# Gated linear attention with a SwiGLU gate: four F blocks ahead instead of five, masked states and key sums by PSUM bank, one reciprocal for a query tile's factors, and the first down weights split without waiting

## The chip, the cores and the metric

The kernel runs on one core of one Trainium2 chip. The time is device microseconds from start to end of one execution; the figure for the kernel before is the median of three runs, 1640.54 us (1640.27 to 1640.99). TensorE multiplies matrices out of SBUF into PSUM (eight banks). VectorE, ScalarE and GpSimd work elementwise; GpSimd cannot reach PSUM. DMA transfers are issued from the queues of SP, ScalarE and GpSimd. Each engine carries out its own instructions in a fixed order and waits on semaphores for the others.

## The reference

One sequence of S = 2048 rows with D = 576 columns, H = 32 heads of 18, and a feed-forward width F = 4608.

```
xn = layernorm(x)
# A: linear attention with a feature map of two softmaxes
q, k, v = split(xn @ wqkv)                      # 32 heads of 18
pq, pk = q @ w_phi, k @ w_phi                   # per head
phi_q = concat(softmax(pq), softmax(-pq))       # 36 features
phi_k = concat(softmax(pk), softmax(-pk))
kv = sum over rows of phi_k^T v;  z = sum over rows of phi_k
o  = (phi_q @ kv) / (phi_q @ z + 1e-6)
s  = o @ wo
# B: SwiGLU
g = silu( (silu(xn @ w_gate) * (xn @ w_up)) @ w_down )
out = x + s * g
```

## The kernel before

Every fp32 operand of a large product is split into a rounded part and a rest (`split`, L57: a ScalarE copy for the first, a VectorE subtraction for the second), and three products of the parts replace one. The rows of x are kept transposed in eight tiles X (`XB`), four for each half of the rows. The program has these stages.

**Opening and keys.** Layernorm, transposes, weights folded with w_phi, then `k_tile` for each of 16 row tiles: the products with the key weights, `softmax_parts` (maximum and minimum, two exponentials on ScalarE, the head sums `sm` and their reciprocals on VectorE), and `kv_step`, which adds phi_k^T v into three PSUM banks `kvp` (four 126-wide blocks in the first two, two 72-wide ones in the third). A column of ones beside v gives the key sums z.

**The seam between keys and queries** (L491 to L515). The key sums are copied out of the banks to `zc` (L500, one column at a time), spread over all partitions by matmuls with the identity (L506) and copied to `zb` (L509). The ten state blocks are masked to their heads (`km`, L513) and split into `KVH` and `KVL`.

**Queries** (L559 to L619). For each row tile `q_tile` multiplies with the query weights, takes the softmax parts, forms ez = e times zb, its head sums y, and from them the factors of numerator and denominator; the last operation on e (L577) applies them. `numer` transposes two such tiles (`pt`, L588) and multiplies with the states (`po`, L594); `project` multiplies with wo (`p`, L614), copies the result on ScalarE (`so`, L618) and stores it.

**Gate, up and down.** F is cut into NF = 36 blocks of 128. The first EARLY blocks are computed ahead, in the plain form: `early_tile` makes, for each of four tiles of 512 rows, 14 matmuls of 512 columns for the gate and 14 for the up product (xw, L92), a Silu on ScalarE, a product on VectorE, and stores h to DRAM. These blocks are given out as filler for TensorE beside the attention stages; the last of them (L1020, L1026) stands between the last projection and the gate stage. All other blocks go through `gate_up` (L727), which computes both products for both tiles of one half of the rows with seven products of seven matmuls (L706) instead of eight; its weights are loaded to `ld`, combined on GpSimd (`ts`, L693 to L696), split to `w`, and kept in DRAM (`w_dram`) for the second half of the rows. In the first two of them (`opening` 0 and 1) the sum xp is copied to SBUF by ScalarE (`snap`, L735) before the next product may add to it. The down product works on pairs of blocks, again by seven products (`strassen`): GpSimd forms the differences of h and of the down rows (`td`, L916 to L923), `prep` splits them to `hh` and `dw`, and `item` multiplies (`pd`, L831).

The program is written with tiles; a scheduler puts each engine's instructions in an order of its own, by priority and by when it expects operands. `tc.high_priority()` lifts an instruction in that order, `tc.issue_after(x)` holds one back until x has been placed. The first down rows lie in the space of `acc` (`first_rows`, loaded at L1024), and for the first step of the first pairs `prep` holds all VectorE work back behind `anchor`, the last product of a gate block:

```
with tc.issue_after(anchor[-1].ins) if first and i == 0 and part == 0 else ExitStack():
    for n, g in enumerate(pairs):
        h, w = f(g)
        hs.append(split_h(h))
        split(w2[:, n, 0], w2[:, n, 1], w)
```

Of the kernel before, what the change touches and what calls it, by code (L numbers as in the profile page):

```python
# [17 lines left out]
P = 128  # L18
# [11 lines left out]
EARLY = 5  # L30
# [7 lines left out]
def heads(ap):  # L38
    return ap.rearrange("p (h d) -> p h d", d=DH)
# [7 lines left out]
def gated_hedgehog_kernel(ctx: ExitStack, tc, x, w_qk, w_v, w_phi, wo, w_gu, w_tail, w_down, ident_in, mask_in, out):  # L47
# [78 lines left out]
    with ExitStack() as att:  # L126
# [9 lines left out]
        with ExitStack() as wst:  # L136
# [136 lines left out]
            def softmax_parts(ps, e):  # L273
# [12 lines left out]
                nc.vector.reciprocal(sm, sm)  # L286
# [114 lines left out]
            def k_tile(t):  # L401
                i0, j0, cols = block(t)
                pk = kps.tile([P, 2, 512], F32, name="p2")
                for i in range(2):
                    w = slice(i * HALF, (i + 1) * HALF)
                    xw(pk[:, i, 0:HALF], i0, j0, cols, KVWH[:, :, :, w], KVWL[:, :, :, w], True)
                phi = kk.tile([P, 2 * D], F32, name="phi", bufs=2)
                sm = softmax_parts(pk, phi)
                nc.vector.tensor_mul(heads(phi), heads(phi), spread(sm, 2 * H))
                return phi  # L410
# [80 lines left out]
        with ExitStack():  # L491
# [4 lines left out]
            zc = qc.tile([GW, 2 * NG], F32, name="zc")  # L496
            for i in range(3):
                for j in range(4 if i < 2 else 2):
                    w = GROUPS[(4 * i + j) // 2][1]
                    nc.scalar.copy(zc[0:w, 4 * i + j:4 * i + j + 1], kvp[i][0:w, j, w:w + 1])  # L500
            for s in range(2):
                for a, m, name in ((0, 4, ("p2", "vw")[s]), (4, 1, ("vy", "vx")[s])):
                    o, w = GROUPS[a]
                    zp = kps.tile([P, 512], F32, name=name)
                    for g in range(a, a + m):
                        nc.tensor.matmul(zp[:, (g - a) * GW:(g - a) * GW + w],  # L506
                                         zc[0:w, 2 * g + s:2 * g + s + 1].to_broadcast([w, P]), ident[0:w, 0:w],
                                         start=True, stop=True)
                    nc.scalar.copy(zb[:, s * D + o:s * D + o + m * w], zp[:, 0:m * w])  # L509
            for i in range(2 * NG):  # L510
                o, w = GROUPS[i // 2]
                km = qc.tile([GW, GW], F32, name="km", bufs=2)
                nc.vector.tensor_mul(km[0:w, 0:w], kvp[i // 4][0:w, i % 4, 0:w],  # L513
                                     mask.rearrange("p h d -> p (h d)")[0:w, 0:w])
                split(KVH[0:w, i, 0:w], KVL[0:w, i, 0:w], km[0:w, 0:w])  # L515
# [7 lines left out]
        with ExitStack() as qst:  # L523
# [35 lines left out]
            def q_tile(t):  # L559
                i0, j0, cols = block(t)  # L560
                pq = qps.tile([P, 2, 512], F32, name="p2")
                for i in range(2):
# [3 lines left out]
                r = softmax_parts(pq, e)  # L566
# [4 lines left out]
                nc.vector.tensor_mul(y, y, r)  # L571
                den = qk.tile([P, H], F32, name="den")
                nc.vector.scalar_tensor_tensor(den, y[:, 0:H], DEN_EPS, y[:, H:], op0=ALU.add, op1=ALU.add)
                nc.vector.reciprocal(den, den)
                nc.vector.tensor_mul(r.rearrange("p (s h) -> p s h", s=2), r.rearrange("p (s h) -> p s h", s=2),
                                     den.unsqueeze(1).to_broadcast([P, 2, H]))
                last_e.append(nc.vector.tensor_mul(heads(e), heads(e), spread(r, 2 * H)))  # L577
# [20 lines left out]
            def project(b, oh, ol, last):  # L598
                for j in range(QS // P):
# [3 lines left out]
                    for i in range(2):  # L603
# [14 lines left out]
                        nc.scalar.copy(so, ps[:, 0:HALF])  # L618
# [273 lines left out]
    def strassen(i, pairs, part, first):  # L892
# [65 lines left out]
        for f in ((p1, p7), (p4, p5, p6, p2, p3))[part]:  # L958
            hs, ws = [], []

            def prep(f=f, hs=hs, ws=ws):
                w2 = fq.tile([P, 2, 2, HALF], F32R, name="dw", bufs=3)
                with tc.issue_after(anchor[-1].ins) if first and i == 0 and part == 0 else ExitStack():
                    for n, g in enumerate(pairs):
                        h, w = f(g)
                        hs.append(split_h(h))
                        split(w2[:, n, 0], w2[:, n, 1], w)
                        ws.append(w2[:, n])
# [134 lines left out]
```

## Time and profile before

| | |
|---|---|
| median of three runs | 1640.54 us |
| profiled execution | 1640.45 us, its span 1638.7 us |
| mean granted TensorE clock | 0.997 |
| keys to queries, the first query matmul | at 232.4 us |
| end of the last projection | at 488.8 us |
| first matmul of the gate, up and down stage | at 513.5 us |

A line of the groups gives the source line, the engine, the operation, the tile written and those read, shapes and count, then busy us, mean ns of one, and idle time before with what ended it. A line of a timeline begins with its start in us from the span's start and its duration; a bracket at its end holds the idle time of the engine before it and what ended that. A line of the view of waits gives who waited for whom, then us in total, times, and the longest. A line of the view by windows gives, for a stretch, the busy time of TensorE, its weight loads, VectorE, ScalarE and GpSimd with their counts, then the granted TensorE clock, the DMA share and GB/s. Matmuls are pipelined, so that their recorded durations overlap.

### The profile page before, as it was taken

The numbers are of one execution on the slowest core, as the hardware profiler recorded it, in microseconds if no ns is written. First come the engines' busy times: TensorE is split into PE (matmuls) and PEld (weight loads), VectorE is DVE, ScalarE is ACT, GpSimd is POOL, SyncE is SP. The second block draws the span as 40 slices with busy tenths as digits, with TensorE's granted clock in tenths as the row PEclk, the third lists the DMA queues.
The fourth block names the chain that finished last, engine by engine and source line by source line (L and its number), as shares of the span: only waits on it lengthen the run. The fifth ranks groups of instructions, "written<-read, shape, count | busy, mean of one in ns | idle before, by whom it ended". The sixth has DMA issues, their size and how long they took to land.

```text
span 1638.7 us, 25220 instructions
## 1 busy us (share of the span) xinstructions
PE 1604.5 (98%) x9385; PEld 1429.4 (87%) x9385; DVE 1175.5 (72%) x1735; ACT 723.8 (44%) x1407; POOL 655.3 (40%) x699
## 2 busy tenths in 40 slices
PE   6999999999999999999999999999999999999997
PEld 5899997999988888888888888888888888888886
DVE  7667768989863778778777778825676766666578
ACT  5533344454433554544444544455433333333334
POOL 3385661342303455455545355313233323133132
PEclk9999999999999999999999999999999999999999
DMA  8622234433329545555554454685454655555445
GB/s 285 206 80 78 78 130 128 117 112 96 93 94 330 202 167 175 178 178 168 179 181 164 174 197 152 223 293 149 140 162 130 201 182 177 166 181 180 140 115 174
DMA packets 121741, 268.47 MB, mean 164 GB/s; under 512 B 12786, under 2 KB 53362, under 8 KB 119826
## 3 DMA queue, kind: packets, MB, share of 16 engines
q1 hardware_dynamic: 106652, 246.49, 46.0%
q0 software_dynamic: 3072, 11.02, 2.5%
q10 hardware_dynamic: 11894, 9.35, 1.8%
q8 instruction: 74, 1.21, 0.3%
q14 instruction: 49, 0.40, 0.1%
HBM read 167.19 MB, written 99.61 MB: 163 GB/s over the span
## 4 chain that ended last, share of the span: by engine, by line
PE 90%; DVE 3%; DMA 3%; POOL 1%; issue 1%; ACT 1%; SPq 0%; ACTq 0%; POOLq 0%; DVEq 0%
PE px L706 24%; PE pd L831 24%; PE pw L706 12%; PE py L706 6%; PE p L92 6%; PE pe L92 5%; PE p L614 4%; PE po L594 2%; PE kvp L295 2%; PE vx L383 1%; PE pt L588 1%; PE vw L383 1%; DMA sraw<-in_A_w_v 1%; DMA xn<-in_A_x 1%; DMA x_dram<-xr 1%
## 5 line engine op out<-in xcount | busy, mean ns | idle before, releaser
L831 PEld LDWEIGHTS pd<-dw,hh 128*128 128x128 f32 x3048 | 432.4, 188 | 26.2 <-DVE dw L59 2.9
L831 PE MATMUL pd<-dw,hh 128*128 128x288 f32 x3048 | 448.5, 297 | 3.8 <-DVE dw L59 2.1
L706 PE MATMUL px<-X,w 128*128 128x512 f32 x1488 | 384.4, 393 | 0.2 <-ACT s L735 0.2
L706 PEld LDWEIGHTS px<-X,w 128*128 128x128 f32 x1488 | 270.6, 188 | 52.2 <-ACT s L735 2.4
L706 PE MATMUL pw<-X,w 128*128 128x512 f32 x732 | 188.7, 393 | 0.0
L706 PEld LDWEIGHTS pw<-X,w 128*128 128x128 f32 x732 | 137.0, 189 | 30.5
L740 DVE TENSOR_TENSOR s<-pw,s 128x512 f32<-128x512 f32 x124 | 85.0, 687 | 101.0 <-ACT s L735 90.3
L956 DVE TENSOR_TENSOR acc<-pd,acc 128x576 f32<-128x576 f32 x128 | 96.2, 752 | 83.6 <-PE pd L831 83.5
L735 ACT COPY s<-px 128x512 f32<-128x512 f32 x124 | 72.6, 585 | 158.3 <-PE px L706 158.3
L92 PE MATMUL pe<-X,wh 128*128 128x512 f32 (+1 forms) x380 | 121.5, 401 | 5.2 <-ACT h L119 2.1
L59 DVE TENSOR_TENSOR hh<-ha,hh 128x512 fp32r<-128x512 f32 x140 | 110.0, 811 | 21.0 <-ACT hh L58 19.5
L58 ACT CAST hh<-ha 128x512 fp32r<-128x512 f32 x140 | 82.7, 619 | 93.1 <-PE pd L831 72.0
L928 POOL TENSOR_TENSOR hb<-hb 128x512 f32<-128x512 f32 x34 | 46.6, 1369 | 164.5 <-DVE hb L752 160.1
L59 DVE TENSOR_TENSOR w<-ld,w 128x512 fp32r<-128x512 f32 (+1 forms) x93 | 77.4, 834 | 34.9 <-ACT w L58 33.8
L706 PE MATMUL px<-X,wt 96*128 96x512 f32 x248 | 97.9, 395 | 0.0
L706 PE MATMUL py<-X,w 128*128 128x512 f32 x372 | 96.7, 394 | 0.0
L915 POOL TENSOR_TENSOR h<-ha,hb 128x512 f32<-128x512 f32 x34 | 44.5, 1310 | 125.6 <-DVE ha L756 88.6
L941 POOL TENSOR_TENSOR ha<-ha 128x512 f32<-128x512 f32 x34 | 52.6, 1563 | 102.5 <-DVE hh L59 102.5
L58 ACT CAST w<-ld 128x512 fp32r<-128x512 f32 (+1 forms) x93 | 50.9, 549 | 88.0 <-POOL ld L696 56.2
L92 PEld LDWEIGHTS pe<-X,wh 128*128 128x128 f32 (+1 forms) x380 | 69.8, 189 | 20.8 <-DVE h L122 3.2
L693 POOL TENSOR_TENSOR ts<-ld 128x256 f32<-128x256 f32 x31 | 27.0, 871 | 139.4 <-issue 70.1
L760 ACT COPY py<-px 128x512 f32<-128x512 f32 x62 | 35.5, 572 | 102.3 <-PE px L706 84.8
(267 smaller groups left out, 3252.2 us busy)
## 6 DMA issues: line engine op xcount, KB each, us to landing
w_dram<-w SPq DMA_DIRECT2D x90, 512.0 KB, 2.9
w<-w_dram SPq DMA_DIRECT2D x90, 512.0 KB, 4.4
wt<-t_dram SPq DMA_DIRECT2D x61, 336.0 KB, 3.7
ld<-in_B_w_gu SPq DMA_DIRECT2D x31, 512.0 KB, 4.5
X<-sum_dram SPq DMA_DIRECT2D x8, 1280.0 KB, 12.2
rt<-in_B_w_down SPq DMA_DIRECT2D x33, 288.0 KB, 3.1
rb<-in_B_w_down SPq DMA_DIRECT2D x33, 288.0 KB, 4.5
w_dram<-w SPq DMA_DIRECT2D x30, 256.0 KB, 2.2
```

What stands on the lines that cost most here:

```text
L58: nc.scalar.copy(hi, src)
L59: nc.vector.tensor_sub(lo, src, hi)
L92: last = nc.tensor.matmul(ps, l, r, start=n == 0, stop=n == len(pairs) - 1)
L614: nc.tensor.matmul(ps[:, 0:HALF], a[0:w, g, jc], bw[0:w, g, n], start=k == 0, stop=k == 3 * NG - 1)
L706: nc.tensor.matmul(ps, l, r, start=first and n == 0, stop=last and n == len(mm) - 1, skip_group_check=True)
L735: nc.scalar.copy(t, ps)
L740: nc.vector.tensor_add(t, ps, t)
L831: nc.tensor.matmul(ps, l, r, start=first and n == 0 and m == 0, stop=n == len(hs) - 1 and m == 2, skip_group_check=True)
L915: sub(s, g["h"][0][0], g["h"][0][1])
L928: nc.gpsimd.tensor_add(a21, a21, g["h"][1][1])
L941: sub(a12, a12, g["h"][0][0])
L956: nc.vector.tensor_add(a2, pd[:, :, 0:HALF], a2)
```

## The change

Five things are changed:

- EARLY is 4 instead of 5: block 4 is computed in the gate and up stage, in both halves of the rows, and block 3 takes its place between projection and gate stage.
- The key sums are copied out by bank (three copies), spread into two adjacent banks and a third (`p2`, `vw`), and copied to `zb` in two copies; the states are masked and split by bank, in one `km` tile.
- `softmax_parts` returns head sums; `k_tile` takes their reciprocal, and `q_tile` works with the sums s of both softmaxes: with y0, y1 the sums of ez, the common denominator is y0 s1 + y1 s0 + 1e-6 s0 s1, one reciprocal of it is taken, and each half's factor is the other half's sum times that.
- The copies `so` of the last projection have high priority.
- In the first `prep`, the split of h stays behind `anchor`, and that of the weights only for the second pair.

```
-EARLY = 5
+EARLY = 4
...
                 sm = kk_pool.tile([P, 2 * H], F32, name="sm")
                 nc.vector.reduce_sum(sm, heads(e), axis=AX.X)
-                nc.vector.reciprocal(sm, sm)
                 return sm
...
                 sm = softmax_parts(pk, phi)
+                nc.vector.reciprocal(sm, sm)
...
-            zc = qc.tile([GW, 2 * NG], F32, name="zc")
-            for i in range(3):
-                for j in range(4 if i < 2 else 2):
-                    w = GROUPS[(4 * i + j) // 2][1]
-                    nc.scalar.copy(zc[0:w, 4 * i + j:4 * i + j + 1], kvp[i][0:w, j, w:w + 1])
-            for s in range(2):
-                for a, m, name in ((0, 4, ("p2", "vw")[s]), (4, 1, ("vy", "vx")[s])):
-                    o, w = GROUPS[a]
-                    zp = kps.tile([P, 512], F32, name=name)
-                    for g in range(a, a + m):
-                        nc.tensor.matmul(zp[:, (g - a) * GW:(g - a) * GW + w],
-                                         zc[0:w, 2 * g + s:2 * g + s + 1].to_broadcast([w, P]), ident[0:w, 0:w],
-                                         start=True, stop=True)
-                    nc.scalar.copy(zb[:, s * D + o:s * D + o + m * w], zp[:, 0:m * w])
-            for i in range(2 * NG):
-                o, w = GROUPS[i // 2]
-                km = qc.tile([GW, GW], F32, name="km", bufs=2)
-                nc.vector.tensor_mul(km[0:w, 0:w], kvp[i // 4][0:w, i % 4, 0:w],
-                                     mask.rearrange("p h d -> p (h d)")[0:w, 0:w])
-                split(KVH[0:w, i, 0:w], KVL[0:w, i, 0:w], km[0:w, 0:w])
+            zc = qc.tile([GW, 12], F32, name="zc")
+            m4 = mask.rearrange("p h d -> p (h d)")
+            banks = [(i, 4 if i < 2 else 2, GROUPS[2 * i][1]) for i in range(3)]
+            for i, n, w in banks:
+                nc.scalar.copy(zc[0:w, 4 * i:4 * i + n], kvp[i][0:w, 0:n, w])
+            zp, zq = kps.tile([P, 2, 512], F32, name="p2"), kps.tile([P, 512], F32, name="vw")
+            for g, (o, w) in enumerate(GROUPS):
+                for s in range(2):
+                    d = zp[:, s, o:o + w] if g < NG - 1 else zq[:, s * w:s * w + w]
+                    nc.tensor.matmul(d, zc[0:w, 2 * g + s:2 * g + s + 1].to_broadcast([w, P]), ident[0:w, 0:w],
+                                     start=True, stop=True)
+            z2, o = zb.rearrange("p (s n) -> p s n", s=2), GROUPS[-1][0]
+            nc.scalar.copy(z2[:, :, 0:o], zp[:, :, 0:o])
+            nc.scalar.copy(z2[:, :, o:D], zq[:, 0:2 * (D - o)].rearrange("p (s n) -> p s n", s=2))
+            for i, n, w in banks:
+                km = qc.tile([GW, 4, GW], F32, name="km")
+                nc.vector.tensor_mul(km[0:w, 0:n, 0:w], kvp[i][0:w, 0:n, 0:w],
+                                     m4[0:w, 0:w].unsqueeze(1).to_broadcast([w, n, w]))
+                split(KVH[0:w, 4 * i:4 * i + n, 0:w], KVL[0:w, 4 * i:4 * i + n, 0:w], km[0:w, 0:n, 0:w])
...
-                r = softmax_parts(pq, e)
+                r = softmax_parts(pq, e).rearrange("p (s h) -> p s h", s=2)
...
-                nc.vector.tensor_mul(y, y, r)
+                y2 = y.rearrange("p (s h) -> p s h", s=2)
+                nc.vector.scalar_tensor_tensor(y2[:, 0], r[:, 0], DEN_EPS, y2[:, 0], op0=ALU.mult, op1=ALU.add)
+                nc.vector.tensor_mul(y2, y2, r[:, ::-1])
                 den = qk.tile([P, H], F32, name="den")
-                nc.vector.scalar_tensor_tensor(den, y[:, 0:H], DEN_EPS, y[:, H:], op0=ALU.add, op1=ALU.add)
+                nc.vector.tensor_add(den, y2[:, 0], y2[:, 1])
                 nc.vector.reciprocal(den, den)
-                nc.vector.tensor_mul(r.rearrange("p (s h) -> p s h", s=2), r.rearrange("p (s h) -> p s h", s=2),
-                                     den.unsqueeze(1).to_broadcast([P, 2, H]))
-                last_e.append(nc.vector.tensor_mul(heads(e), heads(e), spread(r, 2 * H)))
+                nc.vector.tensor_mul(y2, r[:, ::-1], den.unsqueeze(1).to_broadcast([P, 2, H]))
+                last_e.append(nc.vector.tensor_mul(heads(e), heads(e), spread(y, 2 * H)))
...
-                        nc.scalar.copy(so, ps[:, 0:HALF])
+                        with tc.high_priority() if last else ExitStack():
+                            nc.scalar.copy(so, ps[:, 0:HALF])
...
-                with tc.issue_after(anchor[-1].ins) if first and i == 0 and part == 0 else ExitStack():
-                    for n, g in enumerate(pairs):
-                        h, w = f(g)
+                early = first and i == 0 and part == 0
+                for n, g in enumerate(pairs):
+                    h, w = f(g)
+                    with tc.issue_after(anchor[-1].ins) if early else ExitStack():
                         hs.append(split_h(h))
+                    with tc.issue_after(anchor[-1].ins) if early and n else ExitStack():
                         split(w2[:, n, 0], w2[:, n, 1], w)
-                        ws.append(w2[:, n])
+                    ws.append(w2[:, n])
```

The scheduler's order moves with it. On TensorE, 104 matmuls of early tiles stood between the last projection and the first gate matmul, and 21 stand there now; between the keys and the first gate matmul there were 420 of them and are 308, of which 201 and 182 after the first transposes of query tiles.

ScalarE around the first gate block, before (`py<-px` is the copy of its first product, `s<-px` the copy that its fifth product waits for, w the second block's weights):

```order
L119 ACTIVATE h<-pe 128x512 x3
L760 COPY py<-px 128x512
L58 CAST dw<-acc 128x288
L58 CAST dw<-td 128x288
L58 CAST w_5422<-ts 128x2x256
L735 COPY s<-px 128x512
L58 CAST w_5426<-ld 128x2x256
L747 ACTIVATE py<-py 128x512
```

and after:

```order
L119 ACTIVATE h<-pe 128x512
L58 CAST w_5241<-ld 128x256
L761 COPY py<-px 128x512
L58 CAST dw<-acc 128x288
L58 CAST dw<-td 128x288 x2
L58 CAST w_5233<-ts 128x2x256
L736 COPY s<-px 128x512
L58 CAST w_5237<-ld 128x2x256
```

A second cast of td now stands ahead of the copy `s<-px`, and fewer early Silus ahead of all of them.

GpSimd at the same place, from the second block's weight subtractions on (td from acc are the first down rows), before:

```order
L695 TENSOR_TENSOR ld<-ld 128x256
L696 TENSOR_TENSOR ld<-ld,ts 128x256
L916 TENSOR_TENSOR td<-acc 128x288
L921 TENSOR_TENSOR acc<-acc 128x288
L922 TENSOR_TENSOR td<-acc 128x288
L693 TENSOR_TENSOR ts<-ld 128x256
```

and after:

```order
L696 TENSOR_TENSOR ld<-ld 128x256
L697 TENSOR_TENSOR ld<-ld,ts 128x256
L917 TENSOR_TENSOR td<-acc 128x288
L922 TENSOR_TENSOR acc<-acc 128x288
L923 TENSOR_TENSOR td<-acc 128x288
L924 TENSOR_TENSOR td<-td,acc 128x288
L694 TENSOR_TENSOR ts<-ld 128x256
```

The fourth subtraction of the first down rows has moved ahead of the third block's weights.

ScalarE at the seam between keys and queries, before (zc the key sums, zb their spread form):

```order
L500 COPY zc<-kvp_920 72x1 x2
L58 CAST KVH<-km 126x126
L509 COPY zb<-p_2368 128x504
L509 COPY zb<-vy 128x72
L58 CAST KVH<-km 126x126 x2
L509 COPY zb<-vw 128x504
L509 COPY zb<-vx 128x72
```

and after:

```order
L500 COPY zc<-kvp_918 126x4
L500 COPY zc<-kvp_919 126x4
L58 CAST KVH<-km 126x504
L500 COPY zc<-kvp_920 72x2
L508 COPY zb<-p_2361 128x2x504
L509 COPY zb<-vw 128x2x72
L58 CAST KVH<-km 126x504
```

Copies and casts are fewer and wider, and the banks vy and vx are no longer read here; the first query product, which waited for ScalarE, waits for VectorE.

## The prediction

> **What bounds the kernel now.** I read the page's busy line first, then the waits of TensorE stretch by stretch, then the timelines of the engines around the two seams that the change touches. The busy line:
>
> ```profile
> PE 1604.5 (98%) x9385; PEld 1429.4 (87%) x9385; DVE 1175.5 (72%) x1735; ACT 723.8 (44%) x1407; POOL 655.3 (40%) x699
> ```
>
> TensorE is busy in 98% of the span. Its waits, in four calls of the view of waits (230 to 300, 300 to 520, 510 to 570, and from 570 us to the end):
>
> ```profile
> PE pe L92 <- DVE h L122: 1.7, 1, 1.7
> PE pt L588 <- DVE e L577: 1.3, 1, 1.3
> PE p L92 <- ACT zb L509: 1.1, 1, 1.1
> PE pe L92 <- ACT h L119: 0.7, 1, 0.7
> ```
> ```profile
> PE p L614 <- ACT so L618: 0.7, 1, 0.7
> ```
> ```profile
> PE pd L831 <- DVE dw L59: 2.1, 2, 1.2
> PE px L706 <- ACT s L735: 0.2, 1, 0.2
> ```
> ```profile
> PE pd L831 <- ACT pd L852: 0.7, 1, 0.7
> PE pd L831 <- ACT acc L802: 0.6, 1, 0.6
> PE pd L831 <- DVE X L956: 0.4, 1, 0.4
> ```
>
> So the query stage and the whole gate, up and down stage run at TensorE's own pace; what can be won there is matmuls that are no longer issued. Waits stand only where the stages meet: 4.8 us between keys and queries (first four rows), 0.7 at the last projection, 2.3 at the opening of gate, up and down. The change touches all three.
>
> **What one matmul costs.** Durations in the records overlap, so I take the pace. Two neighbouring early tiles are 28 matmuls of 512 columns apart, and their Silu on ScalarE shows the distance:
>
> ```profile
> 503.88 0.60 ACT L119 ACTIVATE h<-pe 128x512 f32<-128x512 f32 x1 [6.16 <-PE pe L92]
> 510.43 0.60 ACT L119 ACTIVATE h<-pe 128x512 f32<-128x512 f32 x1 [5.95 <-PE pe L92]
> ```
>
> 6.55 us for 28, 0.234 us each. The Trainium skill, page "TensorE: Matmul & The Clock Gate", section "Back-to-back issue gap", gives about 131 ns for one of 512 columns in a sustained stream, and 216 ns alone. This trace is above both; by 131 ns the term below would be 1.8 us instead of 3.3.
>
> **1. One block fewer ahead.** A block computed ahead takes 4 tiles of 28 matmuls, 112. The same block by seven products takes 7 x 7 for each half of the rows, 98. So 14 matmuls fall away: 14 x 0.234 = 3.3 us, all on the path, since TensorE waits for nothing else in those stages. The stored h of that block is no longer written and read; its split weights are. ScalarE, VectorE and GpSimd get one more block in each half; the stage from 570 us on has 1.7 us of TensorE waits in all and long stretches with gate and up blocks alone, so I cost that at nothing. If VectorE fell behind there, the waits for X and acc would grow.
>
> **2. Key sums by bank.** Ten one-column copies become three, four copies of the sums two, ten masked products with ten splits three with three. In the order, the first query matmul waited for ScalarE's last copy of sums and now waits for an early tile's VectorE product that is long done. So the 1.1 us wait goes, and the query stage could begin up to 1.9 us earlier (the copies of one column gone as well). But what comes next does not move with it:
>
> ```profile
> 253.51 0.94 ACT L551 CAST th<-tl 128x896 fp32r<-128x896 f32 x1 [1.69 <-POOL tl L550]
> ```
> ```profile
> 257.72 0.50 PE L92 MATMUL pe<-X,wh 128*128 128x512 f32 x1 [0.73 <-ACT h L119]
> ```
>
> ScalarE stands at the tail weights, whose load and GpSimd subtractions do not depend on the sums, and only then comes to the Silu that frees TensorE's bank at 257.7. If TensorE arrives 1.9 us sooner, it waits 2.6 there instead of 0.7. Bounds: 0 to 1.9 us gained; I take 0.3, near the lower end, because that row is the next thing on the path.
>
> **3. One reciprocal.** For a query tile a reciprocal of 64 goes, and an addition of 32 replaces the fused operation's place:
>
> ```profile
> L286 DVE RECIPROCAL sm<-sm 128x64 f32<-128x64 f32 x12 | 6.5, 543 | 0.0
> ...
> L573 DVE SCALAR_TENSOR_TENSOR den<-y 128x32 f32<-128x32 f32 x12 | 2.2, 185 | 0.2
> ```
>
> 0.543 - 0.185 = 0.36 us for a tile, 5.7 us of VectorE over 16 tiles. TensorE has no wait on VectorE after 272.5 us in this stage, so I cost it at 0; it pays for the filler that part 1 takes away (the second rival). The new order also lets a third tile's maxima go ahead of the first tile's factors, which puts the first transposes back behind the same VectorE work: nothing won of the 1.3 us there.
>
> **4. High priority for the last s copies.** ScalarE's order at the last projection is the same before and after (copy, store, first gate weight, copy, copy), so the 0.7 us stays: 0, with 0.7 as the other end.
>
> **5. Down weights not held back.** The two VectorE halves of the first down weights leave the crowd at 538 to 547 us. What remains is the h split ahead of them:
>
> ```profile
> 540.51 0.45 DVE L59 TENSOR_TENSOR dw<-acc,dw 128x288 fp32r<-128x288 f32 x1
> ```
>
> The first wait and the second end one such operation earlier: -0.45 of the 2.1 us.
>
> **6. The cover of the opening.** This is the term that decides. In the order 104 early matmuls stood between the last projection and the first gate matmul; now 21. Everything that this opening needs from memory was hidden under those 104:
>
> ```profile
> 481.14 0.58 SPq L675 DMA_DIRECT2D ld<-in_B_w_gu  x1
> ...
> 492.61 1.88 SPq L1024 DMA_DIRECT2D acc<-in_B_w_down  x2
> ```
> ```profile
> 488.77 0.39 PE L92 MATMUL pe<-X,wl 128*128 128x512 f32 x1
> ...
> 513.50 0.40 PE L744 MATMUL py<-X,w 128*128 128x512 f32 x1
> ...
> 520.18 1.54 PE L706 MATMUL px<-X,w 128*128 128x512 f32 x6
> ```
> ```profile
> 498.41 0.80 POOL L916 TENSOR_TENSOR td<-acc 128x288 f32<-128x288 f32 x1 [2.92 <-DMA acc<-in_B_w_down]
> ...
> 500.17 0.80 POOL L922 TENSOR_TENSOR td<-acc 128x288 f32<-128x288 f32 x1
> ```
> ```profile
> 516.36 0.43 ACT L58 CAST dw<-td 128x288 fp32r<-128x288 f32 x1
> 518.54 0.62 ACT L58 CAST w<-ts 128x512 fp32r<-128x512 f32 x1 [1.75 <-PE px L706]
> 519.06 0.58 ACT L735 COPY s<-px 128x512 f32<-128x512 f32 x1
> ```
>
> On the clock of before: the projection ends at 488.8, 21 x 0.234 = 4.9 us later, at 493.7, the gate block would begin. The large X tiles no longer matter: in the order their loads stand ahead of ld, inside the query stage. The gate weights are just in time (ld at 481.1, 12.6 us earlier). The down rows are not: they reach GpSimd at 498.4. And ScalarE, in program order, now has between the copy py<-px and the copy s<-px one cast of acc, two casts of td (one before) and the cast of w. The second td is GpSimd's fourth subtraction, which part 5 lets go ahead at once. Chain: 500.17 + 0.80 + 0.08 + 0.80 = 501.9 us td; cast 0.43, 502.3; w and s end 1.1 us after w begins (519.06 + 0.58 - 518.54), 503.3. TensorE wants s copied before its fifth product, which begins 520.18 - 513.50 = 6.7 us after py, at 500.4. That is a wait of 3.0 us if the rows land as before. The DMA then carried the X tiles as well, from 497.4 on; without them the rows may land up to about 1.4 us sooner (494.5, when both are issued, plus 2.5, is 497.0). Bounds: 0 (rows at 495.4) and 3.0; I take 2.5, near the upper end, which is the row itself. Behind ScalarE then wait the second block's weights on VectorE and their stores on SP, and SP's fourth gate weight load now stands behind one more store and the two loads of h; but TensorE stands still as long, so I add nothing.
>
> **The sum** against the profiled execution (1640.45 us, 0.1 below the median of the three): -3.3 - 0.3 - 0.45 + 2.5 = -1.55, 1638.9.
>
> **Rivals.**
> The waits are hidden. If the down rows land early enough that s is copied in time, 2.5 goes out of the sum: 1636.4. For it: the DMA of before was shared. Against it: the casts stand ahead of s in the order whatever lands.
>
> The keys-to-queries seam loses its waits. If the tail weights come sooner too, up to all 4.8 us go instead of 0.3: 1634.4; half of them, 1636.8. For it: GpSimd's work ahead of those loads waits for a ScalarE copy that stands behind the key sums. Against it: the row at 253.51.
>
> The query stage starves. It ends slower. Its filler goes from 201 early matmuls after the first transposes to 182, and in before the transposes follow VectorE closely:
>
> ```profile
> 299.19 1.36 DVE L577 TENSOR_TENSOR e<-e,sm 128x1152 f32<-128x1152 f32 x1
> ```
> ```profile
> 301.38 0.81 PE L588 MATMUL pt<-ident,e 128*126 128x128 f32 x6
> ```
>
> 0.8 us of room. If each of the eight steps came 0.8 us late, that is 6.4 us: 1645.3. From 0.6 us a step it is slower than before by more than what a measurement tells. Against it: VectorE loses 5.7 us of work and the splits of one block, TensorE only 4.4 us of matmuls.
>
> The clock gives. After a wait early in the kernel the granted clock fell, at 540 us after a similar one it did not (the clock is the third number from the end):
>
> ```profile
> 16.00:20.00 4.00, 2.17 (x16) 2.10 (x16) 4.00 (x8) 2.28 (x4) 1.75 (x2) 0.90 0.65 242
> 20.00:24.00 4.00, 4.00 (x25) 3.96 (x25) 3.66 (x11) 2.90 (x5) 0.74 (x1) 0.67 0.88 226
> ```
> ```profile
> 540.00:544.00 4.00, 2.05 (x12) 1.62 (x13) 4.00 (x7) 0.62 (x1) 1.47 (x2) 1.00 0.71 237
> ```
>
> A dip of that size costs 4 x 0.10 + 4 x 0.33 = 1.7 us: 1640.6. The Trainium skill, "TensorE: Matmul & The Clock Gate", section "What's actually happening", halves the clock after an idle window of about 3.4 us; by that, a 2.5 us wait would mostly escape.
>
> Nothing is saved. If the fewer matmuls only uncover other waits (the opening loses 3.3 instead of 2.5, the h splits come late), it is 1640 to 1641.
>
> **How the numbers follow.** Forecast 0.35 (own range 1637.5 to 1640.0), waits hidden 0.21, seam without waits 0.16, query stage starved 0.16, clock 0.06, nothing saved 0.06. About 0.2%, 3.3 us, is what a measurement of this kernel tells from no change: faster is 0.21 + 0.16 = 0.37, same 0.35 + 0.06 + 0.06 = 0.47, slower 0.16. The range 1633.5 to 1643.5 leaves out the starved stage and a little below.
>
> **What would show it.** Right: 14 matmuls fewer on TensorE; the wait on zb gone and the wait on ACT h near 257 longer; a wait of px on ACT s of 2 to 3 us some 7 us after the first gate matmul, with casts of td just ahead on ScalarE; pd on dw about 1.6. Wrong: no wait at that px (1636), many small waits of pt on e (slower), or a granted clock below 0.9 after the opening.

## The result and the profile after

The changed kernel is slower: 1645.0 us (median of 14 runs, 1639.9 to 1647.8) against 1639.8 for the kernel before on the same chip (14 runs, 1638.8 to 1641.7). The ratio is 1.0033, 95% interval 1.0026 to 1.0041, so +5.4 us (4.3 to 6.7). The forecast was 1638.9 with a range up to 1643.5, so the time lies outside the range and on the other side of no change. The profiled execution of the changed kernel took 1644.8 us (span 1642.7), 4.0 us above the span of 1638.7 before. One execution of each of two experiments below (6119 and 1752 us) was far longer than all others and is left out of their figures.

TensorE's waits after, in three of the stretches of the prediction (230 to 300, 300 to 520, 510 to 570; from 570 us on they are as before, 0.7, 0.6 and 0.4):

```profile
PE pe L92 <- DVE h L122: 1.6, 1, 1.6
PE pe L92 <- ACT h L119: 1.5, 1, 1.5
PE p L92 <- DVE e L279: 1.4, 1, 1.4
...
PE p L614 <- ACT so L619: 2.9, 2, 2.1
PE px L707 <- ACT s L736: 2.5, 1, 2.5
...
PE pd L832 <- DVE hh L59: 1.8, 1, 1.8
PE pd L832 <- DVE dw L59: 1.5, 1, 1.5
```

The first group is 4.5 us instead of 4.8; the wait on zb is gone and the one on ACT h has grown, as forecast. The px wait is 2.5, to the decimal what was forecast. Two things are not: the wait for so is 2.9 instead of 0.7, and the pd waits are 3.3 instead of 2.1, where 1.65 was forecast.

The so wait, in the order of time (TensorE, then ScalarE, then SP):

```profile
424.33 0.40 PE L614 MATMUL p<-WOH,oh 126*128 126x288 f32 x1
...
426.42 0.38 PE L588 MATMUL pt<-ident,e 128*126 128x128 f32 x2
...
429.15 0.40 PE L614 MATMUL p<-WOH,oh 126*128 126x288 f32 x1 [2.09 <-ACT so L619]
...
432.65 0.69 PE L92 MATMUL p<-QH,X 128*128 128x288 f32 x3
```
```profile
421.11 0.40 ACT L619 COPY so<-p 128x288 f32<-128x288 f32 x1 [1.69 <-PE p L614]
...
423.87 0.40 ACT L619 COPY so<-p 128x288 f32<-128x288 f32 x1 [0.87 <-PE p L614]
...
428.70 0.40 ACT L619 COPY so<-p 128x288 f32<-128x288 f32 x1 [3.85 <-DMA s_dram<-so]
```
```profile
411.13 10.77 SPq L663 DMA_DIRECT2D X<-sum_dram  x2
```

There are two so buffers. The third copy of so waits until the store of the first has landed, and while it waits, TensorE has no bank to project into. The stores land late because two large X loads, issued at 411 to 422 us, are on the DMA; an experiment below moves these loads. In the view of the tile so (380 to 500 us), the time from issue to landing is, before and then after:

```profile
DMA to landing us min/median/max: 1.7/1.8/3.9
```
```profile
DMA to landing us min/median/max: 1.7/6.0/7.0
```

In before those X loads were issued from 497 us on, behind the last store of s. With one block fewer ahead SP issues them inside the query stage.

The clock, in windows of 4 us of the changed kernel (the third number from the end is the granted clock); in before every window from 24 us to the last matmul is at 0.97 or more:

```profile
428.00:432.00 4.00, 2.85 (x13) 2.85 (x14) 3.79 (x8) 0.40 (x1) 1.97 (x4) 0.69 1.01 375
432.00:436.00 4.00, 4.00 (x28) 4.00 (x28) 0.52 (x1) 0.40 (x1) 0.00 (x0) 0.88 0.24 82
...
496.00:500.00 4.00, 1.49 (x7) 1.05 (x6) 1.84 (x3) 2.44 (x5) 1.42 (x3) 1.00 0.92 295
...
520.00:524.00 4.00, 1.68 (x7) 1.45 (x8) 4.00 (x6) 0.62 (x1) 1.86 (x2) 0.71 0.64 210
524.00:528.00 4.00, 4.00 (x13) 3.35 (x13) 0.83 (x3) 1.19 (x3) 0.81 (x1) 0.50 0.00 0
528.00:532.00 4.00, 4.00 (x23) 3.55 (x22) 1.69 (x3) 2.77 (x6) 2.62 (x3) 0.94 0.32 131
```

The clock falls behind the so wait and behind the pd waits, and not behind the px wait of 2.5 us at 496 to 500. (It also stands at 0.70 and 0.88 from 32 to 40 us, but before had 0.90 and 0.67 from 16 to 24, so these two cancel.) What it costs is read from the pace. Fifteen projection matmuls took 426.42 - 424.33 = 2.09 us ahead of the so wait and 432.65 - 429.15 = 3.50 behind it: 1.4 us lost. The second place is costed below against an experiment without the dip: 2.6 us.

So, relative to before: -3.3 for the 14 matmuls (9385 to 9371 in the busy line), -0.3 at the seam, +2.3 px (0.2 to 2.5), +1.2 pd, +2.2 so, +1.4 and +2.6 clock, together +6.1, where the two spans are 4.0 apart. Of the 2.1 us left, 1.0 lies ahead of the last key products, which begin at 225.94 us instead of 226.91, where TensorE's work is still the same; over the profiled executions of this document that start lies between 224.4 and 228.0. Part 2 explains some of the rest (experiments below), and single executions of one kernel differ by more than that.

### The profile page after: what moved, and what is told of

It reads as the page before. It is cut to its first block, busy times and chain, and to the rows that moved or that the text cites. A ratio compares the mean times of both kernels' runs of the same rounds, so it can differ in the third digit from the quotient of the medians.

```text
span 1642.7 us, 25184 instructions
## 1 busy us (share of the span) xinstructions
PE 1605.5 (98%) x9371; PEld 1430.6 (87%) x9371; DVE 1172.9 (71%) x1725; ACT 725.9 (44%) x1399; POOL 657.0 (40%) x703
## 3 DMA queue, kind: packets, MB, share of 16 engines
q8 instruction: 74, 1.21, 0.3%
## 4 chain that ended last, share of the span: by engine, by line
PE 89%; DVE 4%; DMA 3%; POOL 1%; issue 1%; ACT 1%; ACTq 0%; SPq 0%; POOLq 0%; DVEq 0%
PE px L707 25%; PE pd L832 24%; PE pw L707 12%; PE py L707 6%; PE p L92 6%; PE p L614 4%; PE pe L92 3%; PE kvp L294 2%; PE po L594 2%; PE vx L382 1%; PE pt L588 1%; DMA s_dram<-so 1%; DMA xn<-in_A_x 1%; PE vw L382 1%; PE tp L193 1%
## 5 line engine op out<-in xcount | busy, mean ns | idle before, releaser
L707 PE MATMUL px<-X,w 128*128 128x512 f32 x1536 | 397.5, 394 | 2.6 <-ACT s L736 2.5
L707 PEld LDWEIGHTS px<-X,w 128*128 128x128 f32 x1536 | 279.6, 188 | 57.5 <-ACT s L736 5.3
L707 PE MATMUL pw<-X,w 128*128 128x512 f32 x756 | 195.0, 393 | 0.0
L707 PEld LDWEIGHTS pw<-X,w 128*128 128x128 f32 x756 | 141.4, 188 | 31.5
L92 PE MATMUL pe<-X,wh 128*128 128x512 f32 x300 | 97.9, 401 | 5.0 <-ACT h L119 2.4
L707 PE MATMUL px<-X,wt 96*128 96x512 f32 x256 | 101.2, 395 | 0.0
L707 PE MATMUL py<-X,w 128*128 128x512 f32 x384 | 100.8, 397 | 0.0
L707 PEld LDWEIGHTS py<-X,w 128*128 128x128 f32 x384 | 69.7, 190 | 11.7
```

What stands on the lines that cost most here:

```text
L92: last = nc.tensor.matmul(ps, l, r, start=n == 0, stop=n == len(pairs) - 1)
L707: nc.tensor.matmul(ps, l, r, start=first and n == 0, stop=last and n == len(mm) - 1, skip_group_check=True)
```

## The experiments

**Which part costs.** First four blocks ahead alone, in the kernel before; then the changed kernel with five.

```
-EARLY = 5
+EARLY = 4
```

> The kernel before with four blocks ahead instead of five and nothing else. Theory (the fewer blocks cost more than their 14 matmuls, -3.3 us): the large X tiles are loaded inside the query stage, the stores of s land later and so copies stop TensorE for about 2 us, the opening waits, and the clock dips after both: +3 to +5 us over the kernel before, 1643 to 1645. Since the second td cast stays held back here, the wait of px on ACT s should be near 0 and those of pd on dw and hh larger than 3.3. Rival (the other four parts cost the time, four blocks is the gain that was forecast): 1636 to 1638.

Measured: 1650.6 us, ratio 1.006 (1.0047 to 1.0073), +9.8. The direction is the theory's, the size twice what it said. From the waits of this kernel (300 to 490 and 490 to 530 us):

```profile
PE p L614 <- ACT so L618: 4.6, 3, 3.4
...
PE py L744 <- ACT so L618: 3.5, 1, 3.5
...
PE p L614 <- ACT so L618: 1.3, 1, 1.3
```

Waits for so are 9.4 us in all. Two points missed: the pd waits were 1.4 and not over 3.3, and a px wait of 2.6, where nearly none was expected, stood one block later, at 537.

```
-EARLY = 4
+EARLY = 5
```

> The changed kernel with five blocks ahead again, all other parts kept. Theory: as the kernel before or 0.3 to 1.5 us faster (the wait on zb gone, the pd waits 0.45 shorter), 1638.3 to 1639.8; no so wait over 0.7, no clock below 0.95 after 40 us. Rival (the other parts cost): 1642 to 1645.

Measured: 1638.4 us, ratio 0.9987 (0.9978 to 0.9995), 2.1 us faster than before. The time is in the number of blocks ahead and what it sets off; the other four parts save a little together. Two points missed: the so wait was 0.9, and the clock did dip, to 0.69 at 540 to 544 us, behind pd waits of 0.7 and 1.5.

**Is it the so buffers?** The changed kernel with a third buffer.

```
-                        so = qk.tile([P, HALF], F32, name="so", bufs=2)
+                        so = qk.tile([P, HALF], F32, name="so", bufs=3)
```

> The changed kernel with three so buffers instead of two. Theory: a third s copy need not wait for the first store to land; the 2.1 us wait of p on ACT so near 427 and the clock dip behind it (about 1.5 us) go, the opening stays: 3 to 4 us less than the changed kernel, 1641 to 1642. Rival (it is the opening alone that costs; the so wait only moves the wait to the opening): no change, 1644.5 to 1645.5.

Measured: 1638.2 us, ratio 0.9986 (0.9975 to 0.9997). That is 4.7 thousandths below the changed kernel's 1.0033, 7.7 us, twice what was expected of a 2.1 us wait and its dip. Its waits from 300 us to 530, and the one window below 0.97 between 40 us and the last matmul:

```profile
PE p L614 <- ACT so L619: 0.9, 1, 0.9
...
PE px L707 <- ACT s L736: 1.8, 1, 1.8
PE pd L832 <- DVE dw L59: 1.5, 1, 1.5
PE pd L832 <- DVE hh L59: 1.4, 1, 1.4
```
```profile
516.00:520.00 4.00, 2.73 (x10) 2.64 (x11) 2.79 (x4) 0.41 (x1) 1.71 (x2) 0.58 0.26 101
```

The so waits lose 2.0 us and their dip is gone. The opening gains as well. In the changed kernel the last so copies also wait for landings (2.82 and 0.83 us), ScalarE's weight casts stand behind them, SP's stores of these weights behind the casts, and SP issues the down rows after those stores, at 488.12, 0.9 us ahead of the first gate matmul (489.06); here it issues them at 482.35, 3.0 us ahead of it (485.33). So px waits 0.7 less and pd 0.4 less, and the dip there is one window instead of three. The stores that those last copies wait for are on the DMA together with the gate weight loads, issued from 476.4 us on; in before one of the last copies also waited 2.55 us for a landing. So the third buffer takes away waits for stores at two places, and only the one at 427 us stands beside the X loads.

The same edit in the kernel before with four blocks:

> The kernel before with four blocks ahead and three so buffers. Theory (the loss of four blocks ahead is the so copies that wait for stores behind the X loads, 5.9 + 3.5 us of waits in the run with two buffers, and the clock behind them): 8 to 10 us less than with two buffers, 1640 to 1643. Rival (the wait is for DMA that is slow anyway, three buffers only put it off to the opening): 1647 to 1650.

Measured: 1643.3 us, ratio 1.0022 (1.0011 to 1.0032), against 1.006 with two buffers. The direction is the theory's and the rival is out, but the gain is 6.2 us by the ratios, not 8 to 10, and the time lies just above the range: all so waits within the query stage are gone, but 2.4 us of them remain at its end, and px waits 3.1 us at 530, with the clock at 0.70 and 0.50 behind it.

**Is it the X loads that make the stores late?** The changed kernel, with the loads of the large X tiles moved behind the first gate weight load on SP (`lds` holds these loads).

```
+            with ExitStack() if i else tc.issue_after(lds[0].ins):
                 nc.sync.dma_start(... sum_dram[i, :, j] ...)
...
-    xo = operands(0)
     early_tile(EARLY - 1, 0, parts)
     ready = [gate_up_weights(*todo.pop(0))]
+    xo = operands(0)
```

> The changed kernel with the loads of the four large X tiles put behind the first gate weight load, so that they are no longer in the query stage; two so buffers. Theory: the s stores land in about 2 us instead of 6, the wait near 427 and its clock dip are gone (windows 400 to 440 at 1.00); the opening then waits for X, ld and the down rows together, 5 to 10 us: 1646 to 1652. Rival (so copies are late for another reason than the X loads): the so wait stays at 2 us.

Measured: 1649.7 us, ratio 1.0059 (1.0042 to 1.0076). The so wait is 0.5, the stores land in 2.3 us (median), the third copy waits for TensorE and no longer for a store, and the clock stands at 1.00 where it was 0.69; at the opening TensorE waits 6.0 us for an X tile:

```profile
DMA to landing us min/median/max: 1.7/2.3/3.5
```
```profile
425.96 0.40 ACT L619 COPY so<-p 128x288 f32<-128x288 f32 x1 [1.76 <-PE p L614]
...
482.60 0.40 ACT L619 COPY so<-p 128x288 f32<-128x288 f32 x1 [5.22 <-DMA s_dram<-so]
```
```profile
428.00:432.00 4.00, 4.00 (x31) 3.95 (x30) 3.79 (x8) 0.40 (x1) 1.97 (x4) 1.00 0.60 158
```
```profile
PE px L708 <- DMA X<-sum_dram: 6.0, 1, 6.0
```

So the X loads are the cause of the late stores within the query stage. They are not the only cause of late stores: at its end, where one X load and the gate weight loads were issued at 472 to 474 us, a copy still waits 5.22 us for one. (The view of landings cannot hold that store: its longest is 3.5.) With 21 early matmuls ahead of the gate instead of 104 the X loads cost more at the opening, in this place at least, than where they were. A third so buffer is the cheaper way out.

**The opening.** Part 5 undone in the changed kernel.

```
-                early = first and i == 0 and part == 0
-                for n, g in enumerate(pairs):
-                    h, w = f(g)
-                    with tc.issue_after(anchor[-1].ins) if early else ExitStack():
+                with tc.issue_after(anchor[-1].ins) if first and i == 0 and part == 0 else ExitStack():
+                    for n, g in enumerate(pairs):
+                        h, w = f(g)
                         hs.append(split_h(h))
-                    with tc.issue_after(anchor[-1].ins) if early and n else ExitStack():
                         split(w2[:, n, 0], w2[:, n, 1], w)
...
```

> The changed kernel with the down weights held back as before (part 5 undone). Theory: one td cast instead of two stands ahead of s<-px on ScalarE, so that s is copied about 2.3 us earlier and the 2.5 us wait of px goes to 0 to 0.3; the pd waits grow from 3.3 to about 4; 1 to 2 us less than the changed kernel, 1643 to 1644. Rival (the first td is as late as the second; part 5 does save): 0.4 us more than the changed kernel, px wait 2.1 to 2.5.

Measured: 1642.7 us, ratio 1.0013 (1.0005 to 1.0022), 3.3 us below the changed kernel by the ratios, more than the 1 to 2 expected: part 5 costs here. ScalarE in the changed kernel, and then with part 5 undone:

```profile
494.53 0.43 ACT L58 CAST dw<-td 128x288 fp32r<-128x288 f32 x1 [1.35 <-POOL td L917]
497.26 0.43 ACT L58 CAST dw<-td 128x288 fp32r<-128x288 f32 x1 [2.29 <-POOL td L924]
...
498.12 0.58 ACT L736 COPY s<-px 128x512 f32<-128x512 f32 x1
```
```profile
496.25 0.43 ACT L58 CAST dw<-td 128x288 fp32r<-128x288 f32 x1 [1.25 <-POOL td L917]
...
497.12 0.58 ACT L736 COPY s<-px 128x512 f32<-128x512 f32 x1
```

The second td, GpSimd's fourth subtraction, no longer stands ahead of s, and px waits 0.8 us there. A new px wait of 1.5 on ACT py appears a block later, and the pd wait is 3.0, where about 4 was expected. All waits of the opening are 5.6 us instead of 5.8, and the two profiled spans are 1.0 us apart (1641.7 and 1642.7). So the waits do not account for the 3.3 us; the second dip is shallower here (0.78 and 0.79 from 520 to 528 us), but how the rest comes about is open. The second td alone can be put back, with part 5 otherwise kept, here with three so buffers: its cast is held behind the second copy of s (`snaps` holds these copies).

```
-                nc.scalar.copy(t, ps)
+                snaps.append(nc.scalar.copy(t, ps))
...
-                    with tc.issue_after(anchor[-1].ins) if early and n else ExitStack():
+                    late4 = first and i == 0 and f is p4 and n == 0
+                    with tc.issue_after(anchor[-1].ins if early else snaps[1].ins) if early and n or late4 else ExitStack():
                         split(w2[:, n, 0], w2[:, n, 1], w)
```

> The changed kernel with three so buffers, and the cast of the second td (GpSimd's fourth subtraction) put behind the second copy of s on ScalarE. Theory: the wait of px on ACT s (1.8 us with three so buffers) goes to 0 to 0.3, the pd waits stay at about 3; 1.5 to 2.5 us less than with three so buffers alone, 1635.5 to 1637. Rival (the time lost at the opening only moves: pd waits 1.8 longer): no change, 1638.

Measured: 1635.0 us, ratio 0.9967 (0.9955 to 0.9979), 3.1 us below the run with three so buffers alone by the ratios (0.9986), where 1.5 to 2.5 was expected. There is no px wait left, so the casts of td ahead of s were its cause; the pd waits are 0.7 and 1.5, 0.7 less than without the edit, and the clock still falls behind them. The last edit takes the first h split out of VectorE's crowd:

```
-                    with tc.issue_after(anchor[-1].ins) if early else ExitStack():
+                    with tc.issue_after(anchor[-1].ins) if early and n else ExitStack():
                         hs.append(split_h(h))
```

> As the run with three so buffers and the second td put back (1635.0), and the split of the first h of the opening pair no longer held back behind the second gate block's product. Theory (the pd waits of 0.7 and 1.5 us come from VectorE, which has five splits at once there; the clock dip of 512 to 520 us follows them): one split fewer in that crowd, the pd waits go to 0.5 to 1.5 in all and the dip with them: 1633 to 1634.5. Rival (the second wait is for dw behind hh, which stays): no change, 1635.

Measured: 1632.7 us, ratio 0.9946 (0.9932 to 0.996), the fastest of all: 7.8 us below the kernel before by the medians, 8.9 by the ratio. TensorE at the opening's down items, in the changed kernel and then in this one:

```profile
522.85 2.29 PE L832 MATMUL pd<-dw,hh 128*128 128x288 f32 x8 [1.50 <-DVE dw L59]
524.94 2.77 PE L707 MATMUL py<-X,w 128*128 128x512 f32 x6
...
529.82 1.77 PE L832 MATMUL pd<-dw,hh 128*128 128x288 f32 x12
```
```profile
514.42 1.33 PE L832 MATMUL pd<-dw,hh 128*128 128x288 f32 x8 [1.49 <-DVE dw L59]
515.58 1.56 PE L707 MATMUL py<-X,w 128*128 128x512 f32 x6
...
518.81 1.77 PE L832 MATMUL pd<-dw,hh 128*128 128x288 f32 x12
```
```profile
512.00:516.00 4.00, 2.51 (x16) 2.18 (x15) 3.94 (x6) 1.63 (x4) 1.39 (x1) 1.00 0.94 312
516.00:520.00 4.00, 4.00 (x22) 3.46 (x22) 1.68 (x3) 3.01 (x6) 2.03 (x3) 1.00 0.15 61
```

The same 8 down and 14 gate matmuls take 6.97 us at the lowered clock and 4.39 us at full clock: the 2.6 us in the account above. The wait of 1.5 is still there; once the 0.7 ahead of it had gone, no dip followed.

**What fewer blocks save when the waits are away.** The kernel with 1635.0, with five blocks.

> As the run with three so buffers and the second td put back (1635.0), but with five blocks ahead. This is the saving of the fewer blocks with the waits that hid it taken away. Theory (14 matmuls saved, 3.3 us, all on the path): 3 to 3.5 us slower than with four blocks, 1638 to 1638.5. Rival (the saving is offset by the opening whose cover is gone): within 1 us of it, 1634 to 1636.

Measured: 1637.2 us, ratio 0.9984 (0.9975 to 0.9993), against 0.9967 with four. That is 1.7 thousandths, 2.8 us, with intervals of about 2 us on each side; 3.3 was forecast. The two profiled spans (1636.4 and 1633.1) are 3.3 apart, but by the medians, 3.3 and 4.3 us below the kernel before, it would be 1.0. So the theory is nearer, and the rival (within 1 us) is not ruled out.

**The clock by itself.** The kernel before, with the copy of s2 repeated 6 to 11 times in 24 blocks of the second half.

```
...
-        s2 = snap(xp)
+        b = opening - NF
+        s2 = snap(xp, 6 + b % 6 if 3 <= b < 27 else 1)
```

> The kernel before with the copy of s2 repeated 6 to 11 times in 24 blocks of the second half, so that TensorE stands for some us at places where it never stood. This measures the clock by itself. Theory (the clock falls in some of such cases, by where in a fixed raster the wait falls): waits of 1.5 to 3 us are followed by 4 us windows below 0.9 in about half of the cases, waits under 1 us in none, waits over 3.5 us in all. Rival (a threshold of length alone): one length parts those with a dip from those without.

Nearly all the waits that came out were under 1 us, so the theory was hardly tested. The two longest:

```profile
1398.53 1.66 PE L706 MATMUL px<-X,w 128*128 128x512 f32 x6 [1.26 <-ACT s L736]
...
1547.10 1.97 PE L706 MATMUL px<-X,w 128*128 128x512 f32 x6 [2.15 <-ACT s L736]
```

Behind the first the clock stayed at 1.00, behind the second it was 0.53 and 0.61. Its time, 1669.2 us (one execution), is more than these waits explain and was not followed up. With the other runs: no dip behind 2.51 us (changed kernel, 498.75), 1.18 + 0.94 (before, 541 to 543), 1.76 (three so buffers); a dip behind 2.09 (changed kernel, 429), 2.15 (here), 0.72 + 1.51 (five blocks), 1.40 + 1.50 (three so buffers), 1.78 + 1.50 (changed kernel, 521 to 523), 3.54 (four blocks alone, 497). So one threshold of length, the rival, does not part them: 2.51 escaped and 2.09 did not. The plainest case is that of two kernels with the same pair of waits: behind 1.18 + 0.94 the clock stayed at 1.00 in before, and behind 1.21 + 0.94, in the kernel with part 3 alone (539 to 541 us), it fell to 0.68 and 0.89. That a fixed raster in time decides is not shown, though it fits. The runs of the changed kernel point the same way: the one of 14 that took 1639.9 us had a mean clock of 0.998, the other 13 (1644.1 to 1647.8) had 0.993 to 0.997. At the higher clock the changed kernel took no longer than the kernel before.

**Parts 2 and 3 alone**, in the kernel before, each with the edit shown in the diff of the change.

> The kernel before with the key sums by PSUM bank and nothing else. With five blocks ahead, parts 2 to 5 together let the first gate matmul begin at 511.5 us instead of 513.5; which part gave that? Theory (the seam between keys and queries, by the wait on zb that goes): the first gate matmul at about 511.8, 1.5 us less in all. Rival (the forecast, the next wait takes it back): 0 to 0.5 us less.

Measured: 1637.6 us, ratio 0.9985 (0.9975 to 0.9994), 2.5 us less (1.0 to 4.1). The first gate matmul begins at 511.07 instead of 513.50, but 1.4 of these 2.4 us lie ahead of the last key products, where nothing was changed (225.52 instead of 226.91). From 230 to 300 us the wait on zb is gone and the next one has hardly grown; the rows are the wait, the last key products on TensorE and the tail weight cast on ScalarE:

```profile
PE pe L92 <- ACT h L119: 0.9, 1, 0.9
```
```profile
225.52 2.18 PE L295 MATMUL kvp<-v,phi 128*126 128x127 f32 x20
```
```profile
250.98 0.94 ACT L550 CAST th<-tl 128x896 fp32r<-128x896 f32 x1 [1.86 <-POOL tl L549]
```

The cast of the tail weights, which was to hold the place, moved along: here it begins 25.5 us after the last key products did (250.98 - 225.52). In the kernel before, where these began at 226.91, it was 26.6 (253.51 - 226.91):

```profile
226.91 2.18 PE L295 MATMUL kvp<-v,phi 128*126 128x127 f32 x20
```

> The kernel before with one reciprocal for a query tile's factors and nothing else. Theory (VectorE stands on the path of the first transposes, and its shorter chain lets them begin sooner): the 1.3 us wait of pt on e goes, the first gate matmul at about 512.2, 1 to 1.4 us less. Rival (the forecast, VectorE off the path): 0.

Measured: 1639.7 us, ratio 0.9994 (0.9985 to 1.0004). The first gate matmul begins at 511.67 and the wait of pt on e is gone, but a wait of 1.4 of p on VectorE's e stands in its place; whether anything is gained the times do not tell. In the trace nothing is: the last key products begin at 224.44, and from there to the first gate matmul it is 287.2 us, in the kernel before 286.6 (513.50 - 226.91).

## Why the prediction was wrong

**The step that failed** is in part 6: "The large X tiles no longer matter: in the order their loads stand ahead of ld, inside the query stage." The place was read correctly, and it is what does the harm: there they share the DMA with the s stores, whose buffers are two. The stores land in 6.0 us (median) instead of 1.8, TensorE waits 2.9 us for so instead of 0.7, and the clock behind that costs another 1.4. With it fell part 4, "the order the same, so the 0.7 us stays": an unchanged order keeps a wait only if what it waits for lands as before. Undoing part 4 leaves the instructions of every engine and their order as they are, so the part itself is worth nothing, as said. Three buffers took away 7.7 us; with them the kernel stands at 1638.2, where 1638.9 was forecast, though largely by luck: by the account above its waits and its dip come to +0.7 us against before (-3.3, -0.3, +1.6 px, +0.8 pd, +0.2 so, +1.7 clock), while its span is 2.8 us shorter (1635.9). 1.3 of that difference lies ahead of the last key products (225.66), and the rest is not accounted for.

**The clock** was given 0.06 and 1.7 us for one dip, with a px wait in mind. It fell at two other places, and not behind px, and took 1.4 + 2.6 us. The Trainium skill, "TensorE: Matmul & The Clock Gate", section "What's actually happening", names an idle window of about 3.4 us for the fall, and calls that window free-running. Here 2.1 us sufficed once and 2.5 did not, so the measurement decides against the length as a safe limit; the free-running window fits.

**Part 5 and the pd waits.** Forecast -0.45; the pd waits grew by 1.2, with the dip behind them. The two operations did leave the crowd, but what was left of it met a GpSimd subtraction (next section but one). With five blocks ahead and all other parts the pd waits were 2.2 us (0.72 + 1.51), in the kernel before 2.1, so the gain of 0.45 does not show there either; why they are 1.1 longer still with four blocks was not tested. Part 6 had charged the second td to part 5 correctly, and then part 5 was still booked as a gain: undoing it gave 3.3 us, and putting back that td alone 3.1.

**Part 2** was booked at 0.3, since ScalarE's tail weight cast would stay where it was. It moved with the seam: with five blocks ahead part 2 gave 1.1 us by the trace, 2.5 (1.0 to 4.1) by the runs. That was the rival "the seam loses its waits", in part. In the changed kernel the cast begins 26.0 us after the last key products (251.98 - 225.94): four blocks alone had put it back to 27.4 (252.86 - 225.47, from 26.6). So the 0.3 was nearly met there, but by two errors that cancel.

**Right:** 14 matmuls fewer, worth 2.8 us by the ratios for 3.3, within wide intervals; the px wait of 2.5 us with the td casts just ahead of s, and its cause, though the size was in part luck (0.7 of it went with the late so stores); the wait on zb gone and the one on ACT h longer; part 3 within what can be measured. The slower rival, 1645.3, met the time by another mechanism: from 300 us to the end of the query stage no wait of pt on e shows.

## What to carry to other kernels

When an edit takes cover away from the end of a stage, look at which loads move into the stage, and at every store there whose buffer someone waits for: two buffers that suffice at 1.8 us to land do not at 6. Price a wait of 2 us or more on TensorE at up to twice its length, since the clock may fall behind it (here 2.1 us cost 3.5, and 3.3 cost 5.9), and remove small waits that stand next to each other first. If a change loses, look for the one resource that turned its saving into a wait before undoing it: three small repairs turned +5.2 us into -7.8 (medians).

## What the runs showed of the hardware

**A VectorE operation beside GpSimd's stands still.** From the changed kernel, VectorE and then GpSimd:

```profile
497.72 0.46 DVE L59 TENSOR_TENSOR dw<-td,dw 128x288 fp32r<-128x288 f32 x1 [2.02 <-ACT dw L58]
...
521.29 1.51 DVE L59 TENSOR_TENSOR dw<-rt,dw 128x288 fp32r<-128x288 f32 x1
```
```profile
520.84 1.64 POOL L934 TENSOR_TENSOR ha<-hb,ha 128x512 f32<-128x512 f32 x1 [0.63 <-DVE hh L59]
```

An operation of one shape takes 0.46 us when GpSimd is idle and 1.51 when one of its operations runs; it ends at 522.80, 0.32 us after GpSimd's at 522.48. This is most of the pd wait of 1.5 us in the changed kernel. In the fastest kernel that operation took 0.45 us, but a split of h, 0.68 us when alone (at 542.94 us in before), met another subtraction, and the wait was 1.49:

```profile
512.23 1.77 DVE L59 TENSOR_TENSOR hh<-ha,hh 128x512 fp32r<-128x512 f32 x1
```
```profile
512.06 1.39 POOL L916 TENSOR_TENSOR h<-ha,hb 128x512 f32<-128x512 f32 x1 [1.73 <-DVE hb L753]
```

It ends at 514.00, 0.55 us after GpSimd's at 513.45. Both operations end a little less than their own length after GpSimd's, as if they began when it ended. The Trainium skill, "SBUF — State Buffer", section "Who interferes with whom", says that the two engines share a pair of ports under an exclusive lock; the trace agrees, as the operations come later by what is left of GpSimd's and are not slower in proportion.

**A clock dip has a size of its own.** In the changed kernel it lowered the clock to between 0.50 and 0.94 for two or three windows of 4 us, and cost 1.4 us behind a wait of 2.1 and 2.6 behind waits of 3.3. Of one length of wait, some have a dip behind them and some have not.
